# Weights of a query and a gate on 128 partitions, and a V load freed from the gate, in a one-token attention kernel

## The chip, the cores and the metric

One core of one Trainium2 chip. The time is that of one execution on the device in microseconds; lower is better. Each time is that of one execution, and each kernel has one trace, of one profiled execution.

## The reference

One token `x` of 448 values is normalized. From it come a query for 16 heads of 256 and, through a two-layer gate, a vector `g`. The query attends to a cache of 65,536 keys and values per head; the result goes through `wo` and is scaled by `g`.

```python
xn = _layernorm(x)                                   # x: 1 x 1 x 448
q  = (xn @ wq).reshape(1, 1, 16, 256)                # wq: 448 x 4096
scores = einsum("bhqd,bhkd->bhqk", q, k_cache) / 16  # k_cache: 16 x 65536 x 256
s  = einsum("bhqk,bhkd->bhqd", softmax(scores), v_cache) @ wo
g  = silu(silu(xn @ w1) @ w2)                        # w1: 448 x 1792, w2: 1792 x 448
return x + s * g
```

All is bf16. K and V are 1,074 MB, wq and wo 3.67 MB each, w1 and w2 1.61 MB each.

## The kernel before

The cache is cut into 64 blocks, each with two K tiles and two V tiles of 4.19 MB (128 partitions of 32 KB). There are two buffers for K and two for V. SyncE (SP) issues all large loads in one queue, in order, and waits ahead of each until the buffer is free:

```python
def sp_block(i):                       # i = 1 .. 63
    for t in range(2):
        take(sp, kf[t])                # DVE has read K tile t of block i-1
        sp.dma_start(out=Kt[t], in_=src(Kd, i, t)).then_inc(kl[t], 16)
        take(sp, vf[t])                # V buffer t is free
        sp.dma_start(out=Vt[t], in_=src(Vd, i - 1, t)).then_inc(vl[t], 16)
```

V lags K by one block. DVE (VectorE) and ACT (ScalarE) multiply K by the query, block after block; PE (TensorE) multiplies the softmax by V. Before the loop (cut):

```python
DC = 4; DP = D // DC                   # 448 rows on 112 partitions, four each
sp.dma_start(out=W[0:DP, 0:DC*HD], in_=A_wq.rearrange("(p c) n -> p (c n)", c=DC))
for t in range(2): ...                 # the two K tiles of block 0
w12 = Vt[1]                            # w1 and w2 lie in the second V buffer at first
sp.dma_start(out=w12[0:DP, 0:DC*F], in_=B_w1.rearrange("(p c) f -> p (c f)", c=DC))
sp.dma_start(out=w12[:, DC*F:...], in_=B_w2...)
...
for g in range(HD // 512):             # query: 8 groups of 4 matmuls
    for c in range(DC):
        pe.matmul(B, lhsT=xnT[0:DP, c, :], rhs=wq_v[0:DP, c, g*512:(g+1)*512],
                  start=(c == 0), stop=(c == DC-1))
...                                    # wo is loaded over wq
dve_block(0); act_block(0)
pe_rows()                              # waits for the end of DVE's block 0
for f in range(FC):                    # gate: 14 groups of 4 matmuls
    for c in range(DC):
        pe.matmul(ps_h[:, f:f+1], lhsT=w1_v[0:DP, c, f, :], rhs=xnT[0:DP, c, 0:1],
                  start=(c == 0), stop=(c == DC-1))
t = silu(h1s, ps_h, ...)               # ACT and DVE
for f in range(FC):
    pe.matmul(ps_y, lhsT=h1s[:, f:f+1], rhs=w2_v[:, f, :], ...)
pe.nop().then_inc(vf[0], 1)            # first V load may go
act.nop().then_inc(vf[1], 1)           # w1 and w2 are read: second V load may go
t_g = silu(g_f, ps_y, ...)             # ACT and DVE; then the loop begins
```

The first V buffer holds nothing at this time: the wait for `vf[0]` protects no data.

Of the kernel before, what the change touches and what calls it, by code (L numbers as in the profile page):

```python
# [21 lines left out]
def kernel(  # L22
# [15 lines left out]
    P = nc.NUM_PARTITIONS  # L38

    _, _, D = A_x.shape  # L40
    _, H, Sk, Dh = A_k_cache.shape
    F = B_w1.shape[1]
    HD = H * Dh
# [1 line left out]
    NB = Sk // (P * KT * TPB)  # L45
    NBLK = H * NB
    NA = SUB - ND
    DC = 4
    DP = D // DC
    assert DP * DC == D and DP <= P  # L50
    FC = F // P
    assert FC * P == F
    NHA = H * 2
# [7 lines left out]
    pe, dve, act, gp, sp = nc.tensor, nc.vector, nc.scalar, nc.gpsimd, nc.sync  # L61
# [3 lines left out]
    Vt = [pool.tile([P, KT * Dh], bf16, name=f"V{t}") for t in range(TPB)]  # L65
    W = pool.tile([P, max(DC * HD, NHA * D)], bf16, name="W")
    prod = [pool.tile([P, NA, Dh], bf16, name=f"prod{i}") for i in range(2)]
# [13 lines left out]
    ones_row = pool.tile([1, P], bf16, name="ones_row")  # L81
# [7 lines left out]
    xn = pool.tile([1, D], bf16, name="xn")  # L89
    xnT = pool.tile([P, DC, P], bf16, name="xnT")  # L90
    h1e = pool.tile([P, FC], fp32, name="h1e")
# [29 lines left out]
    def mark(e, ins):  # L121
        count[e] += 1
        ins.then_inc(line[e], 1)
        return (e, count[e])

    def need(e, *toks):
        for p, c in toks:
            if seen.get((e, p), 0) < c:
                eng[e].wait_ge(line[p], c)
                seen[(e, p)] = c  # L130

    def sem(name):
        return tc.alloc_semaphore(name)
# [7 lines left out]
    vf = [sem(f"vf{t}") for t in range(TPB)]  # L141
# [5 lines left out]
    dl = {n: sem(f"dl_{n}") for n in ("x", "wq", "w12", "wo", "out")}  # L147
# [156 lines left out]
    def pe_turn():  # L304
# [12 lines left out]
                    ins.then_inc(vf[1], 1)  # L317
        ins.then_inc(ho, 1)

    with tc.tile_critical():  # L320

        act.dma_start(out=x_f[0:1, :], in_=A_x[0, 0:1, :]).then_inc(dl["x"], 16)
        sp.dma_start(
            out=W[0:DP, 0 : DC * HD], in_=A_wq.rearrange("(p c) n -> p (c n)", c=DC)
        ).then_inc(dl["wq"], 16)
        for t in range(TPB):
            sp.dma_start(out=Kt[t][:, :], in_=src(Kd, 0, t)).then_inc(kl[t], 16)
        w12 = Vt[1]
        sp.dma_start(
            out=w12[0:DP, 0 : DC * F], in_=B_w1.rearrange("(p c) f -> p (c f)", c=DC)  # L330
        ).then_inc(dl["w12"], 16)
        sp.dma_start(
            out=w12[:, DC * F : DC * F + FC * D], in_=B_w2.rearrange("(p c) d -> p (c d)", c=FC)
        ).then_inc(dl["w12"], 16)
# [7 lines left out]
        for T, w in ((ident, P), (eye2, 2)):  # L342
            g_o = mark("gp", gp.affine_select(
                out=T[:], in_=T[:], compare_op=ALU.not_equal, fill=1.0, base=0,
# [11 lines left out]
            out=rstd[0:1, :], in_=mv[0:1, 1:2], func=ACT.Sqrt, bias=eps_t[0:1, 0:1], scale=1.0  # L356
# [5 lines left out]
            out=xn[0:1, :],  # L362
# [4 lines left out]
            op1=ALU.mult,  # L367
        ))

        xn_c = xn[0:1, :].rearrange("o (p c) -> o c p", c=DC)  # L370
        ps_xt = ps_a[:, :].rearrange("p (c n) -> p c n", c=DC)
        need("pe", t5, g_c)
        for c in range(DC):
            ins = pe.matmul(
                ps_xt[0:DP, c, :], lhsT=xn_c[0:1, c, :], rhs=ones_row[0:1, :], start=True, stop=True
            )
        t6 = mark("pe", ins)
        need("dve", t6)
        t7 = mark("dve", dve.tensor_copy(out=xnT[0:DP, :, :], in_=ps_xt[0:DP, :, :]))


        wq_v = W[:, 0 : DC * HD].rearrange("p (c n) -> p c n", c=DC)
        need("pe", t7)
        pe.wait_ge(dl["wq"], 16)
        bufs = [ps_a, ps_b]
        free = [None, None]
        for g in range(HD // 512):
            B = bufs[g % 2]
            if free[g % 2]:
                need("pe", free[g % 2])  # L390
            for c in range(DC):
                ins = pe.matmul(  # L392
                    B[:, :],
                    lhsT=xnT[0:DP, c, :],
                    rhs=wq_v[0:DP, c, g * 512 : (g + 1) * 512],
                    start=(c == 0),
                    stop=(c == DC - 1),
                )
            t8 = mark("pe", ins)
            need("act", t8)  # L400
            t9 = mark("act", act.copy(out=qb[:, g * 512 : (g + 1) * 512], in_=B[:, :]))  # L401
            free[g % 2] = t9
# [6 lines left out]
            out=W[:, 0 : NHA * D].rearrange("p (h e) -> p h e", h=H),  # L409
            in_=A_wo.rearrange("(h p a) d -> p h (a d)", p=P, a=2),  # L410
# [9 lines left out]
        w1_v = w12[:, 0 : DC * F].rearrange("p (c q f) -> p c f q", c=DC, f=FC)  # L420
        w2_v = w12[:, DC * F : DC * F + FC * D].rearrange("p (f d) -> p f d", d=D)
        ps_h, ps_y = ps_a[:, 0:FC], ps_b[0:1, 0:D]
        pe.wait_ge(dl["w12"], 32)
        need("pe", t_q)
        for f in range(FC):
            for c in range(DC):
                ins = pe.matmul(
                    ps_h[:, f : f + 1],
                    lhsT=w1_v[0:DP, c, f, :],
                    rhs=xnT[0:DP, c, 0:1],  # L430
                    start=(c == 0),
                    stop=(c == DC - 1),
                )
# [14 lines left out]
        for f in range(FC):  # L448
            ins = pe.matmul(
                ps_y, lhsT=h1s[:, f : f + 1], rhs=w2_v[:, f, :], start=(f == 0), stop=(f == FC - 1)  # L450
            )
        t = mark("pe", ins)
        pe.nop().then_inc(vf[0], 1)
        need("act", t)
        act.nop().then_inc(vf[1], 1)
        t_g = silu(g_f[0:1, :], ps_y, g_e[0:1, :], t)
# [24 lines left out]
        n = [0]  # L481

        def own(ins):
# [16 lines left out]
            out=wgt[:, :, :],  # L500
# [12 lines left out]
            out=cf[:, :, :],  # L513
# [10 lines left out]
            out=cf[:, :, :],  # L524
# [5 lines left out]
        for a in range(2):  # L530
            t = mark("dve", dve.tensor_tensor(  # L531
                out=part[:, :, a, :], in0=hv[:, :, :, 2 + a], in1=cf[:, :, :], op=ALU.mult
# [3 lines left out]
            out=OT32[:, :, :], in_=part[:, :, :, :], axis=AX.X, op=ALU.add  # L536
# [3 lines left out]
            out=OT[:, :], in_=OT32[:, :, :].rearrange("p h a -> p (h a)")  # L540
# [5 lines left out]
        for n in range(NHA):  # L546
            ins = pe.matmul(  # L547
                ps_ao[0:1, :],
                lhsT=OT[:, n : n + 1],
                rhs=wo_n[:, n, :],  # L550
                start=(n == 0),
                stop=(n == NHA - 1),
# [4 lines left out]
            out=tmp[0:1, :], in0=ps_ao[0:1, :], in1=g_f[0:1, :], op=ALU.mult  # L557
# [3 lines left out]
            out=out_bf[0:1, :], in0=tmp[0:1, :], in1=x_f[0:1, :], op=ALU.add  # L561
# [34 lines left out]
```

## Time and profile before

| | before |
|---|---|
| median of 3 runs | 2559.31 us (2557.88 to 2560.91) |
| DMA queue busy | 99% of 16 engines, 432 GB/s from 100 us on |
| DVE, PE busy | 87%, 50% |
| a block: DMA, DVE | 38.8 us, 34.5 us |

DMA is the bound nearly throughout. Only the head, the first 100 us, has anything to give, and there a chain of compute (wq, query, block 0, gate, block 1) decides when buffers come free.

### The profile page before, as it was taken

What the parts mean: (1) busy time and instruction counts of PE and PEld (TensorE: products, weight loads), DVE (VectorE), ACT (ScalarE), POOL (GpSimd) and SP (SyncE); (2) the same over time, 40 slices, a digit from 0 to 9 for tenths busy, and PEclk for the clock granted to TensorE, in tenths of its full rate; (3) what the DMA queues carried; (4) which work ended last, traced back from release to release, by engine and by line L of the source; (5) the groups of instructions that cost most, each with busy time, mean ns of one, the idle gap of its engine ahead of it and who ended that gap; (6) DMA issues with size and microseconds to landing.
All of it is one profiled execution on the core that took longest, in us unless ns stands there. A gap on an engine that the chain in (4) does not pass through costs nothing. (4 is left out here: it accounts for less than half of the span.)

```text
span 2558.7 us, 30403 instructions
## 1 busy us (share of the span) xinstructions
PE 1278.9 (50%) x4876; PEld 477.5 (19%) x4876; DVE 2218.3 (87%) x10263; ACT 1445.5 (56%) x6990; POOL 1.2 (0%) x11
## 2 busy tenths in 40 slices
PE   1554554555455445445545544554554454455456
PEld 0211211111112112112111111121121121121112
DVE  5888988988988988889889889889888898898894
ACT  4556555555655555556565555556555565655552
POOL 0000000000000000000000000000000000000000
PEclk7676777677767767776777777777777777777768
DMA  9999999999999999999999999999999999999995
GB/s 350 404 433 430 432 433 430 431 433 431 430 434 431 431 433 431 431 433 432 430 433 432 430 432 432 430 432 432 431 432 433 430 433 433 429 433 433 429 433 223
DMA packets 39343, 1084.43 MB, mean 424 GB/s; under 512 B 4162, under 2 KB 6212, under 8 KB 6212
## 3 DMA queue, kind: packets, MB, share of 16 engines
q1 hardware_dynamic: 39330, 1084.31, 99.0%
q8 instruction: 3, 0.05, 0.0%
q14 instruction: 8, 0.07, 0.0%
q10 hardware_dynamic: 2, 0.00, 0.0%
HBM read 1084.29 MB, written 0.00 MB: 424 GB/s over the span
## 5 line engine op out<-in xcount | busy, mean ns | idle before, releaser
L241 ACT ACTIVATE junk_a<-prod 128x256 bf16<-128x256 bf16 x3328 | 1330.7, 401 | 755.8 <-ACTq L136 755.8
L288 PE MATMUL psO<-V,PV 128*2 128x512 bf16 x4096 | 1169.5, 456 | 1105.8 <-PEq L136 1105.8
L206 DVE CUSTOM_DVE_ANT_0 junk_d<-K,qcur 128x256 bf16<-128x256 bf16 x4864 | 1698.8, 413 | 0.0
L288 PEld LDWEIGHTS psO<-V,PV 128*2 128x2 bf16 x4096 | 389.2, 96 | 1859.7 <-issue 1526.2
L192 DVE TENSOR_TENSOR prod<-K,qcur 128x3328 bf16<-128x3328 bf16 x256 | 482.8, 1886 | 243.5 <-DVEq L136 243.4
L241 ACT ACTIVATION_READ_ACCUMULATOR junk_a<-prod 128x1 f32 x3328 | 620.3, 186 | 0.0
L206 DVE DVE_READ_ACCUMULATOR2_ANT S<- 128x1 f32 x4864 | 365.9, 75 | 0.0
L272 ACT COPY O<-psO 2x512 f32<-2x512 f32 x64 | 36.7, 574 | 217.3 <-ACTq L136 217.3
L309 PE MATMUL ps_t<-eye,O 2*128 2x1 f32 x512 | 68.5, 251 | 49.6 <-PEq L136 49.6
L309 PEld LDWEIGHTS ps_t<-eye,O 2*128 2x128 f32 x512 | 64.9, 191 | 69.9 <-issue 69.8
L274 ACT COPY hist<-ps_t 128x2 f32 x64 | 10.2, 160 | 90.9 <-ACTq L136 90.9
L182 DVE COPY qcur<-qb 128x256 bf16 (+1 forms) x64 | 14.5, 227 | 38.6 <-ACT qb L401 23.0
L278 PE MATMUL ps_nb<-gmax,ones_row 1*128 1x1 bf16 x64 | 10.1, 158 | 62.3 <-PEq L136 62.0
L299 PE MATMUL ps_m<-ident,rmax 128*1 128x128 bf16 x64 | 14.1, 220 | 36.8 <-PEq L136 36.8
L261 ACT ACTIVATE PV<-S,hist 128x128 bf16<-128x128 f32 x64 | 25.7, 402 | 2.1
L223 DVE COPY S<-S 128x128 f32<-128x128 f32 x64 | 14.5, 227 | 9.3
L497 DVE TENSOR_REDUCE negM<-hist 128x16 f32<-128x64 f32 x1 | 0.3, 265 | 22.7 <-ACT hist L274 22.7
L171 DVE TENSOR_REDUCE gmax<-ps_m 1x1 bf16<-1x128 f32 x64 | 17.6, 275 | 1.6 <-DVEq L136 1.6
L278 PEld LDWEIGHTS ps_nb<-gmax,ones_row 1*128 1x128 bf16 x64 | 6.0, 94 | 66.2 <-issue 66.0
L224 DVE TENSOR_REDUCE rmax<-S 128x1 bf16<-128x128 f32 x64 | 18.0, 281 | 0.0
L299 PEld LDWEIGHTS ps_m<-ident,rmax 128*1 128x1 bf16 x64 | 5.4, 84 | 45.9 <-issue 37.8
L401 ACT CAST qb<-ps_a 128x512 bf16<-128x512 f32 x4 | 2.3, 585 | 18.0 <-PE ps_a L392 18.0
(55 smaller groups left out, 79.7 us busy)
## 6 DMA issues: line engine op xcount, KB each, us to landing
K<-in_A_k_cache_dram SPq DMA_DIRECT2D x128, 4096.0 KB, 21.3
V<-in_A_v_cache_dram SPq DMA_DIRECT2D x128, 4096.0 KB, 28.7
W<-in_A_wq_dram SPq DMA_DIRECT2D x1, 3584.0 KB, 17.1
W<-in_A_wo_dram SPq DMA_DIRECT2D x1, 3584.0 KB, 30.3
V<-in_B_w_dram SPq DMA_DIRECT2D x2, 1568.0 KB, 44.5
x_f<-in_A_x_dram ACTq DMA_DIRECT2D x1, 0.9 KB
out_dram<-out_bf SPq DMA_DIRECT2D x1, 0.9 KB
```

The source lines that it names most:

```text
L171: dve.reduce_max(out=gmax[0:1, :], in_=ps_m[0:1, :], axis=AX.X).then_inc(gm, 1)
L182: q_t = own(dve.tensor_copy(out=qcur[:, :], in_=qb[:, sub(q0, Dh)]))
L192: m = dve.tensor_tensor(out=prod[k % 2][:, :, :], in0=Kv[:, s * SUB + ND : (s + 1) * SUB, :], in1=qcur[:, None, :].to_broadcast([P, NA, Dh ...
L206: ins = dve.tensor_tensor_reduce(out=junk_d[jk][:, :], in0=Kv[:, s * SUB + j, :], in1=qcur[:, :], scale=1.0, scalar=0.0, op0=ALU.mult, op1 ...
L224: dve.reduce_max(out=rmax[:, :], in_=S[:, :], axis=AX.X).then_inc(rm, 1)
L241: ins = act.activation(out=junk_a[jk][:, :], in_=prod[k % 2][:, j, :], func=ACT.Identity, accum_out=S[:, a : a + 1],)
L261: act.activation(out=PV[:, :], in_=S2[:, :], func=ACT.Exp, bias=neg, scale=scale, accum_out=hist[:, at(i), 1:2].rearrange("p o s -> p (o s)"),
L272: act.copy(out=O[:, :], in_=psO[:, :]).then_inc(oc, 1)
L278: pe.matmul(ps_nb[:, 0:1], lhsT=ones_row[0:1, :], rhs=gmax[0:1, :], start=True, stop=True).then_inc(bm, 1)
L288: ins = pe.matmul(psO[:, :], lhsT=PV[:, t * KT + 2 * c : t * KT + 2 * c + 2], rhs=Vt[t][:, c * 2 * Dh : (c + 1) * 2 * Dh], start=(t == 0 a ...
L299: pe.matmul(ps_m[0:1, :], lhsT=rmax[:, 0:1], rhs=ident[:, :], start=True, stop=True).then_inc(tm, 1)
L309: ins = pe.matmul(ps_t[:, a : a + 1], lhsT=Ov[:, j, a, :], rhs=eye2[:, j : j + 1], start=(j == 0), stop=(j == 1),)
```

## The change

The intent: load wq and w1 with 128 partitions (three rows each, 384 rows) and a rest of 64 rows, since 112 partitions load slowly here (283 GB/s in the stretch of wq, beside 421 to 433 in those of the K tiles with 128); and let the first V load go at once.

```diff
-    DC = 4
-    DP = D // DC
+    DF = D // P            # 3
+    DR = D % P             # 64
+    DC = DF + 1
...
+    def load_rows(T, M, w, s):
+        sp.dma_start(out=T[:, 0 : DF*w], in_=M[0 : DF*P].rearrange("(p c) n -> p (c n)", c=DF)).then_inc(s, 16)
+        sp.dma_start(out=T[0:DR, DF*w : DC*w], in_=M[DF*P : D]).then_inc(s, 16)
+    def rows(c):
+        return slice(0, P if c < DF else DR)
...
+        sp.sem_inc(vf[0], 1)
+        load_rows(W, A_wq, HD, dl["wq"])
...
-                    lhsT=xnT[0:DP, c, :],
-                    rhs=wq_v[0:DP, c, g * 512 : (g + 1) * 512],
+                    lhsT=xnT[rows(c), c, :],
+                    rhs=wq_v[rows(c), c, g * 512 : (g + 1) * 512],
...
-                    lhsT=w1_v[0:DP, c, f, :],
-                    rhs=xnT[0:DP, c, 0:1],
+                    lhsT=w1_v[rows(c), c, f, :],
+                    rhs=xnT[rows(c), c, 0:1],
...
-        pe.nop().then_inc(vf[0], 1)
```

(The transposition of `xn` follows the same rows, and the waits count the added loads.)

More of the change, by code (lines that the diff above doesn't have):

```diff
@@ L47 @@
     NA = SUB - ND
-    DC = 4
-    DP = D // DC
-    assert DP * DC == D and DP <= P
+    DF = D // P
+    DR = D % P
+    DC = DF + 1
     FC = F // P
@@ L318, in pe_turn @@
         ins.then_inc(ho, 1)
+    def load_rows(T, M, w, s):
+        sp.dma_start(
+            out=T[:, 0 : DF * w], in_=M[0 : DF * P].rearrange("(p c) n -> p (c n)", c=DF)
+        ).then_inc(s, 16)
+        sp.dma_start(out=T[0:DR, DF * w : DC * w], in_=M[DF * P : D]).then_inc(s, 16)
+    def rows(c):
+        return slice(0, P if c < DF else DR)
     with tc.tile_critical():
         act.dma_start(out=x_f[0:1, :], in_=A_x[0, 0:1, :]).then_inc(dl["x"], 16)
-        sp.dma_start(
-            out=W[0:DP, 0 : DC * HD], in_=A_wq.rearrange("(p c) n -> p (c n)", c=DC)
-        ).then_inc(dl["wq"], 16)
+        sp.sem_inc(vf[0], 1)
+        load_rows(W, A_wq, HD, dl["wq"])
         for t in range(TPB):
@@ L328 @@
         w12 = Vt[1]
-        sp.dma_start(
-            out=w12[0:DP, 0 : DC * F], in_=B_w1.rearrange("(p c) f -> p (c f)", c=DC)
-        ).then_inc(dl["w12"], 16)
+        load_rows(w12, B_w1, F, dl["w12"])
         sp.dma_start(
@@ L368 @@
         ))
-        xn_c = xn[0:1, :].rearrange("o (p c) -> o c p", c=DC)
+        xn_c = xn[0:1, 0 : DF * P].rearrange("o (p c) -> o c p", c=DF)
         ps_xt = ps_a[:, :].rearrange("p (c n) -> p c n", c=DC)
@@ L374 @@
             ins = pe.matmul(
-                ps_xt[0:DP, c, :], lhsT=xn_c[0:1, c, :], rhs=ones_row[0:1, :], start=True, stop=True
+                ps_xt[rows(c), c, :],
+                lhsT=xn_c[0:1, c, :] if c < DF else xn[0:1, DF * P : D],
+                rhs=ones_row[0:1, :],
+                start=True,
+                stop=True,
             )
@@ L378 @@
         need("dve", t6)
-        t7 = mark("dve", dve.tensor_copy(out=xnT[0:DP, :, :], in_=ps_xt[0:DP, :, :]))
+        dve.tensor_copy(out=xnT[:, 0:DF, :], in_=ps_xt[:, 0:DF, :])
+        t7 = mark("dve", dve.tensor_copy(out=xnT[0:DR, DF, :], in_=ps_xt[0:DR, DF, :]))
         wq_v = W[:, 0 : DC * HD].rearrange("p (c n) -> p c n", c=DC)
         need("pe", t7)
-        pe.wait_ge(dl["wq"], 16)
+        pe.wait_ge(dl["wq"], 32)
         bufs = [ps_a, ps_b]
@@ L422 @@
         ps_h, ps_y = ps_a[:, 0:FC], ps_b[0:1, 0:D]
-        pe.wait_ge(dl["w12"], 32)
+        pe.wait_ge(dl["w12"], 48)
         need("pe", t_q)
```

## The prediction

Its times for the loads of 64 rows (2.4 us in the 9.7 of part (a)'s landing, some 1 us in the 4.2 of part (b), the 1.2 us lost in the sum for DMA alone) were the author's estimate; no trace had shown them.

> **What bounds the kernel now.** I read the page first, for the slices of the span and the DMA queues.
>
> ```profile
> DMA  9999999999999999999999999999999999999995
> GB/s 350 404 433 430 432 433 430 431 433 431 430 434 431 431 433 431 431 433 432 430 433 432 430 432 432 430 432 432 431 432 433 430 433 433 429 433 433 429 433 223
> ...
> q1 hardware_dynamic: 39330, 1084.31, 99.0%
> ```
>
> The 16 DMA engines are busy 99% of the time at 430 to 433 GB/s from the third slice on (a slice is 64 us). 1084.3 MB at 432 GB/s are 2510 us of a span of 2558.7. So the bound is the traffic of the K and V tiles; DVE, at 87% busy, is close behind. Only the first two slices (350 and 404 GB/s) and the last one run below this rate. The change touches the first two only, so I cut them into stretches (the view of busy time by stretches; the last two columns are the DMA share and GB/s).
>
> ```profile
> 2.00:18.20 16.20, 0.68 (x4) 0.49 (x4) 2.01 (x5) 1.58 (x2) 0.16 (x2) 1.00 1.04 283
> 18.20:36.00 17.80, 10.03 (x32) 3.55 (x32) 7.04 (x31) 9.47 (x32) 0.00 (x0) 0.86 0.98 421
> 36.00:48.00 12.00, 0.00 (x0) 0.00 (x0) 12.00 (x51) 5.84 (x31) 0.00 (x0) 0.50 0.98 300
> 48.00:58.00 10.00, 0.00 (x0) 0.00 (x0) 10.00 (x50) 6.93 (x35) 0.00 (x0) 0.50 1.12 414
> 58.00:64.50 6.50, 1.01 (x15) 0.90 (x16) 5.19 (x30) 4.89 (x20) 0.00 (x0) 0.50 0.98 423
> 64.50:74.00 9.50, 7.42 (x60) 4.13 (x58) 0.99 (x5) 0.71 (x2) 0.00 (x0) 0.60 0.64 245
> 74.00:99.00 25.00, 8.62 (x33) 2.99 (x33) 24.67 (x96) 13.10 (x65) 0.00 (x0) 0.73 1.01 433
> ```
>
> Three stretches are slow. In 2 to 18 and in 36 to 48 the engines are busy (1.04, 0.98) and yet slow (283, 300 GB/s): transfers that are inefficient in themselves. In 64.5 to 74 they are idle (share 0.64). Up to 74 us, 24.9 MB have moved (each length times its rate, summed); at 432 GB/s that is 57.6 us, so the head has lost 16.4 us.
>
> Next the SyncE queue in order of time, for which transfers these are and what holds back the next.
>
> ```profile
> 0.97 0.40 SPq L323 DMA_DIRECT2D W<-in_A_wq_dram  x1
> 1.42 0.89 SPq L327 DMA_DIRECT2D K<-in_A_k_cache_dram  x2
> ...
> 28.31 0.38 SPq L408 DMA_DIRECT2D W<-in_A_wo_dram  x1
> 46.29 3.63 SPq L165 DMA_DIRECT2D K<-in_A_k_cache_dram  x1
> 68.54 0.34 SPq L167 DMA_DIRECT2D V<-in_A_v_cache_dram  x1
> 69.14 0.33 SPq L165 DMA_DIRECT2D K<-in_A_k_cache_dram  x1
> 73.16 0.33 SPq L167 DMA_DIRECT2D V<-in_A_v_cache_dram  x1
> 95.35 0.33 SPq L165 DMA_DIRECT2D K<-in_A_k_cache_dram  x1
> ```
>
> Transfers follow the order of issue: wq in the first slow stretch; then two K tiles; w1 and w2 in the second; then wo and one K tile. Then nothing is queued until the V load at 68.54, which waits for the gate's last matmul to be reached on PE; the K load behind it (69.14) waits in the same queue. That is the idle stretch.
>
> Last, the timeline, for the compute chain beside this.
>
> ```profile
> 18.25 1.86 PE L392 MATMUL ps_a<-W,xnT 112*128 112x512 bf16 x4 [13.01 <-DMA W<-in_A_wq_dram]
> ...
> 28.93 0.23 DVE L182 COPY qcur<-qb 128x256 bf16<-128x256 bf16 x1 [22.96 <-ACT qb L401]
> ...
> 63.48 0.27 PE L299 MATMUL ps_m<-ident,rmax 128*1 128x128 bf16 x1 [35.21 <-PEq L136]
> ...
> 77.83 0.23 DVE L182 COPY qcur<-qb 128x256 bf16 x1 [0.26 <-issue]
> ```
>
> PE stands 13.01 us for wq. The query takes 10.7 us (18.25 to 28.93), DVE's first block 34.5 us (to 63.4), the gate 14.4 us (to 77.83), and only then DVE starts block 1; halfway through it, 17.5 us later, it frees the K tile that is reloaded at 95.35. No DVE operation in this chain waits for DMA once wq is there.
>
> [...] I add the times of the 128-row and the 64-row load.
>
> **The change part by part.**
>
> (a) wq, 3.67 MB. Now it is 128 rows of 24,576 B (3.15 MB) and 64 rows of 8,192 B (0.52 MB). At 432 GB/s the first is 7.3 us[...]. For start and landing I use a load into an empty queue, the V load of 68.54:
>
> ```profile
> V<-in_A_v_cache_dram SPq DMA_DIRECT2D x1, 4096.0 KB, 13.6
> ```
>
> Its 4.19 MB are 9.7 us at 432, so 3.9 us are start and landing. Landing is 0.97 + 3.9 + 9.7 = 14.6, against 18.1 (0.97 + 17.1, the page's list of DMA issues). So everything that follows wq on the compute chain moves 3.5 us earlier. The same number of matmuls runs (32 for the query, 56 for w1, by the comparison of the instruction order), with 128 rows in place of 112; [...] I give this no time. One DVE copy more (some 0.3 us, before wq is there) is hidden.
>
> (b) w1, 1.61 MB: [...] with w2 (1.61 MB, 128 rows, 3.7 us) 7.9 us in place of the 12-us stretch, in which some wo was moved too: 3 to 4 us saved. Nobody waits for w1 before 63: only DMA time.
>
> (c) The V load has its buffer free from the start, so SyncE issues it behind the K load, at some 43 to 47 us, and the next K load as soon as the first block ends (about 60). The idle stretch closes. It is worth 16 us (58 to 74) minus 5.08 MB / 432 GB/s = 11.75, so 4.25 us.
>
> **DMA alone** would gain: wq 16.2 us of the first stretch for 4.58 MB (10.6 at 432), less [...] some 0.5 of start, so about 4; w1 3 to 4; idle 4.25; 11 to 12 us in all. It does not get them, because of the next buffer. Now three tiles (V, K, V) follow the restart at 68.54: 12.58 MB, of which the stretches of 2 us show 1.72 MB by 74; the other 10.86 at 433 are 25.1 us, to 99.1. The K load at 95.35 comes before that, so DMA never notices. After the change the three tiles would be through by 99.1 - 11.5 = 87.6, but the K load of block 2 is released by DVE, whose chain moved 3.5 us only: 95.35 - 3.5 = 91.85. **DMA will run dry** for some 4 us there, and a restart costs 1.5 us (from 68.54 to 74 it moved 1.72 MB, 4.0 us' worth, in 5.46). K of block 2 effectively starts at 93.35 in place of 99.1: a gain of **5.8 us**. Behind it two tiles (K, V) cover 19.4 us, and the next K load comes 17.1 us after (112.47 - 95.35 now), so no second gap. From there both kernels stream at 432, and DVE, with 34.5 us a block against 38.8 for four tiles (16.8 MB), catches up. The gain is carried to the end: 2559.3 - 5.8 = 2553.5.
>
> Taken singly by the same working: the layout alone shifts everything by 3.5 us; the V load alone closes the idle time to 95.35 + 1.5 = 96.85, a gain of 2.3. They add.
>
> **Rivals.**
> 1. DMA's 11.5 us come through in full (2547.8). For it: 99% busy DMA. Against: the gap at 88 to 92 worked out above; it would need K of block 2 released by 87.6.
> 2. [...] 128 rows do not help because the slow start is something else (first access to memory, five transfers mixing). Then DVE's chain does not move, and only the V load pays: 2.3 us, 2557. Against it: w1 is slow too, at 300 GB/s, far from any start, and has the same 112 rows.
> 3. The early V load delays something: it precedes K of block 1's second half, which DVE needs at about 91; with 9.7 us a tile it lands near 80. Nothing is lost. Were wo or w1 behind it, the gate would wait; they are ahead of it in the queue.
> 4. The bound goes to DVE for good. No: 34.5 against 38.8 us a block; it decides one release only.
>
> **Range and chances.** Wq's landing is uncertain by 1.5 us, the restart by 1, and runs of one kernel differ by 1.5 either way (2557.88 to 2560.91). That gives 2553.5 with 2549.5 to 2557. Two per cent are 51 us, more than the whole head; nothing in the steady state is touched.
>
> **What would show it.** wq landing at 14 to 15 us (first query matmul 14.7 in place of 18.25); DVE's first copy of the query near 25.4; the first V issue before 50, the K behind it near 60; 58 to 74 us at some 430 GB/s; block 1 on DVE from 74.3; the K load of block 2 near 91.8 with a dip of DMA share just before it; 432 GB/s and the same tail thereafter. I am wrong if wq lands after 17, if no dip shows near 88 to 92, or if the steady rate moves by 1 GB/s (5.8 us).

## The result, and the profile after

The changed kernel took 2557.76 us (median of 4, 2556.17 to 2558.72) beside 2560.11 of the kernel before. A ratio is the mean time of one kernel's fast runs over that of the other's of the same rounds, so not quite the ratio of the medians: 0.9991, with an interval of 0.9974 to 1.0009. A second measurement gave 0.9998 (below). So the gain is 0.5 to 2.3 us, and not clear of noise, where 5.8 were forecast with a range down to 2.3 (2557.0); the median lies outside it.

First the stretches of the head in the kernel after (length, then busy time of PE, weight loads, DVE, ACT, GpSimd, then clock, DMA share, GB/s). The last row is from a finer cut.

```profile
2.00:18.20 16.20, 3.80 (x11) 1.03 (x11) 2.07 (x6) 2.16 (x3) 0.16 (x2) 1.00 1.03 374
...
36.00:48.00 12.00, 0.00 (x0) 0.00 (x0) 12.00 (x53) 6.49 (x32) 0.00 (x0) 0.50 1.02 356
...
64.50:74.00 9.50, 8.53 (x51) 5.21 (x51) 0.59 (x3) 0.19 (x1) 0.00 (x0) 0.51 0.98 419
74.00:99.00 25.00, 11.77 (x49) 4.22 (x47) 23.55 (x87) 12.11 (x59) 0.00 (x0) 0.73 0.71 295
...
91.00:97.00 6.00, 6.00 (x29) 2.35 (x28) 6.00 (x35) 4.47 (x23) 0.00 (x0) 1.00 0.01 5
```

All three slow stretches of the kernel before are better: 374 GB/s in place of 283, 356 in place of 300, 419 in place of 245. Summed over the prediction's stretches (length times rate; the rows cut here have 416, 431 and 449 GB/s), the changed kernel is 4.05 MB ahead at 74 us, which is 9.4 us' worth at 432 GB/s. And nearly all of it is lost again at one place: from 74 to 99 the rate is 295 where it was 433, because between 91 and 97 us next to nothing is loaded (5 GB/s, before 421). At 99 us 0.60 MB are left, 1.4 us' worth. The queue says what DMA waits for there.

```profile
1.07 0.42 SPq L321 DMA_DIRECT2D W<-in_A_wq_dram  x1
1.54 0.56 SPq L324 DMA_DIRECT2D W<-in_A_wq_dram  x1
...
45.14 0.37 SPq L165 DMA_DIRECT2D K<-in_A_k_cache_dram  x1
45.78 0.34 SPq L167 DMA_DIRECT2D V<-in_A_v_cache_dram  x1
62.23 0.33 SPq L165 DMA_DIRECT2D K<-in_A_k_cache_dram  x1
74.68 0.33 SPq L167 DMA_DIRECT2D V<-in_A_v_cache_dram  x1
96.86 0.33 SPq L165 DMA_DIRECT2D K<-in_A_k_cache_dram  x1
```

The V load goes at 45.78 in place of 68.54, as intended. The K tile of block 2 is issued at 96.86: 1.5 us later than before (95.35), where 91.85 was predicted. Its buffer is freed by DVE, halfway through block 1. So the chain, in order of time:

```profile
15.14 1.97 PE L404 MATMUL ps_a<-W,xnT 128*128 128x512 bf16 x4 [9.84 <-DMA W<-in_A_wq_dram]
...
27.77 0.23 DVE L182 COPY qcur<-qb 128x256 bf16<-128x256 bf16 x1 [21.68 <-ACT qb L413]
...
62.33 0.27 PE L299 MATMUL ps_m<-ident,rmax 128*1 128x128 bf16 x1 [35.22 <-PEq L136]
62.53 5.96 PE L439 MATMUL ps_a<-xnT,V 128*128 128x1 bf16 x56
...
79.35 0.23 DVE L182 COPY qcur<-qb 128x256 bf16 x1 [0.26 <-issue]
```

(The row of x56 merges 42 matmuls of 128 rows and 14 of 64.) Stage by stage, from these lines and those of before:

| stage | before, us | after, us | difference |
|---|---|---|---|
| first query matmul at | 18.25 | 15.14 | -3.11 |
| query, to DVE's copy | 10.68 | 12.63 | +1.95 |
| block 0 | 34.55 | 34.56 | 0 |
| gate, to DVE's next copy | 14.35 | 17.02 | +2.67 |
| half of block 1, to the K issue | 17.52 | 17.51 | 0 |
| K of block 2 issued at | 95.35 | 96.86 | +1.51 |

wq comes 3.1 us earlier, and then PE gives up 4.6 us in the query and the gate. In the gate nearly all of it is one row; in the kernel before it was

```profile
63.68 3.52 PE L427 MATMUL ps_a<-xnT,V 112*128 112x1 bf16 x56
```

The same 56 matmuls, 3.52 us before and 5.96 after. The weight loads show what is different. Kernel before, the first group of the query (PEld is a weight load; in brackets the idle time ahead of it):

```profile
18.22 0.14 PEld L392 LDWEIGHTS ps_a<-W,xnT 112*128 112x128 bf16 x2 [13.17 <-issue]
18.25 1.86 PE L392 MATMUL ps_a<-W,xnT 112*128 112x512 bf16 x4 [13.01 <-DMA W<-in_A_wq_dram]
18.63 0.15 PEld L392 LDWEIGHTS ps_a<-W,xnT 112*128 112x128 bf16 x1 [0.28 <-issue]
19.06 0.15 PEld L392 LDWEIGHTS ps_a<-W,xnT 112*128 112x128 bf16 x1 [0.28 <-issue]
19.48 0.15 PEld L392 LDWEIGHTS ps_b<-W,xnT 112*128 112x128 bf16 x1 [0.28 <-issue]
```

and the kernel after:

```profile
15.53 0.15 PEld L404 LDWEIGHTS ps_a<-W,xnT 128*128 128x128 bf16 x1 [0.28 <-issue]
16.51 0.10 PEld L404 LDWEIGHTS ps_a<-W,xnT 64*128 64x128 bf16 x1 [0.84 <-issue]
17.05 0.13 PEld L404 LDWEIGHTS ps_b<-W,xnT 128*128 128x128 bf16 x2 [0.44 <-issue]
```

Before, a weight load follows the last by 0.43 us and lies beside the matmul ahead of its own. After, the load of 64 rows stands idle for 0.84 us, and the first of 128 rows behind it for 0.44: each starts only when the matmul ahead of its own is nearly at its end (the trace's ends of matmuls are modelled). The loads themselves take no longer: in w1 0.13 us with 64 rows and 0.15 on average with 128, beside 0.16 with 112 before. From the starts of single matmuls in the trace, a group of four costs 0.86 us before and 1.07 after at PE's fast rate in the query (1.71 and 1.93 at its slow rate), and 0.24 and 0.42 in w1. (PE has two rates: in the kernel before, the 512-column matmuls follow each other by 0.43 us until 24.2 us and by 0.22 from there on. The expectations call them cold and warm, and the change to the fast one the warm-up.) So passing from 128 rows to 64 and back costs 0.18 to 0.22 us. Eight groups of the query and 14 of w1 make 8 x 0.21 + 14 x 0.18 = 4.2 us of the 4.6. For the query this is an upper estimate: part of its 1.95 us is that PE became fast later, 7.6 us after the first matmul in place of 5.9 (see r12).

That was the theory to test. The late weight loads agree with it (0.84 us idle ahead of the load of 64 rows, in place of 0.28); what in PE makes the pass cost time is not shown by any trace. The prediction had not looked for such a cost.

### The profile page after: what moved, and what is told of

It reads as the page before. It is cut to its first block, busy times and chain, and to the rows that moved or that the text cites. A ratio compares the mean times of both kernels' runs of the same rounds, so it can differ in the third digit from the quotient of the medians.

```text
span 2556.9 us, 30406 instructions
## 1 busy us (share of the span) xinstructions
PE 1283.2 (50%) x4876; PEld 478.6 (19%) x4876; DVE 2218.3 (87%) x10264; ACT 1445.4 (57%) x6990; POOL 1.2 (0%) x11
## 5 line engine op out<-in xcount | busy, mean ns | idle before, releaser
L261 ACT ACTIVATION_READ_ACCUMULATOR PV<-S,hist x64 | 11.9, 186 | 0.0
## 6 DMA issues: line engine op xcount, KB each, us to landing
W<-in_A_wo_dram SPq DMA_DIRECT2D x1, 3584.0 KB, 26.2
W<-in_A_wq_dram SPq DMA_DIRECT2D x1, 3072.0 KB, 11.5
V<-in_B_w_dram SPq DMA_DIRECT2D x1, 1344.0 KB, 34.1
W<-in_A_wq_dram SPq DMA_DIRECT2D x1, 512.0 KB, 13.5
V<-in_B_w_dram SPq DMA_DIRECT2D x1, 224.0 KB, 35.6
```

Source lines behind the costliest of these rows:

```text
L261: act.activation(out=PV[:, :], in_=S2[:, :], func=ACT.Exp, bias=neg, scale=scale, accum_out=hist[:, at(i), 1:2].rearrange("p o s -> p (o s)"),
```

## The experiments

Theory P: the passes lengthen the chain, the chain releases the K tile of block 2 late, DMA runs dry. Rivals: R, 128 rows are slower than 112 in themselves; L, the addresses of the new layout are slower to load as weights; D, DMA gives the saving back in the steady state; G, the layout is worth nothing anyway, and only the gate's place matters.

| run | median | before beside it | ratio (95%) | K of block 2 issued | last K of the loop issued |
|---|---|---|---|---|---|
| before | | | | 95.35 | 2480.69 |
| after | 2557.76 | 2560.11 | 0.9991 (0.9974 to 1.0009) | 96.86 | 2478.61 |
| r1 after again | 2558.45 | 2559.47 | 0.9998 (0.9985 to 1.0012) | 96.64 | 2478.04 |
| r2 layout only | 2562.08 | 2559.47 | 1.0008 (0.9994 to 1.0022) | 97.59 | 2482.18 |
| r3 early V only | 2557.85 | 2559.47 | 0.9994 (0.9981 to 1.0008) | 94.06 | 2478.72 |
| r4 padded | 2553.02 | 2559.47 | 0.9975 (0.9961 to 0.9988) | 90.66 | 2471.99 |
| r7 zigzag | 2555.79 | 2560.15 | 0.9982 (0.9968 to 0.9996) | 94.26 | 2475.47 |
| r8 padded, gate off | 2552.29 | 2560.15 | 0.9969 (0.9955 to 0.9983) | 80.21 | 2471.36 |
| r9 before, early V, gate off | 2558.55 | 2559.46 | 0.9996 (0.9983 to 1.0010) | 86.05 | 2477.32 |
| r10 after, gate off | 2551.74 | 2559.46 | 0.9972 (0.9958 to 0.9985) | 80.06 | 2470.99 |
| r11 padded, w1 ahead | 2552.12 | 2559.46 | 0.9970 (0.9957 to 0.9984) | 86.74 | 2471.89 |

Runs r1 to r4 shared one chip and its runs of before, so did r5 to r8, and r9 to r12. Every result was found correct, but for r5, r6 and r12 this says only that the tolerance did not notice the rows left out. These three were run once each, for their traces: 2568.69, 2560.21 and 2568.17 us.

**r1: the changed kernel again.**

> The changed kernel once more, on the chip of the next three, so that they can be compared with it. Theory P (PE pays for the pass between 128-row and 64-row matmuls, and the chain through the gate and DVE releases the K tile of block 2): 1.5 to 3 us faster than before, K of block 2 issued at 96.9 us, DMA empty for some 6 us before it. Rival D (the gain is small because DMA gives it back later, in the steady state): the rate between 100 and 2500 us is lower than in the kernel before by some 3 us' worth.

The time is 1.0 us better than before by the medians, less than the 1.5 to 3 of theory P. The trace repeats: K of block 2 at 96.64, 299 GB/s from 74 to 99. The steady state is 432 GB/s from 99 us to 2500 in both kernels, and the last K load of the loop comes 2.65 us earlier than in the kernel before. Rival D falls: what is gained at 100 us is still there at 2478.

**r2: the layout alone, and r3: the early V load alone.** In r2 the line `sp.sem_inc(vf[0], 1)` goes and `pe.nop().then_inc(vf[0], 1)` returns; in r3 the kernel before gets the opposite edit.

> The new layout alone; the V load waits for the gate again. Theory P: the first query matmul near 15.1, but the gate's second matmul group only near 69.5 (68.2 before), so the three tiles that wait for it start 1.3 us later than before and nothing else limits: 1 to 1.5 us slower than before, in spite of wq and w1 taking 7 us less DMA time. My recorded working (layout shifts the chain): 3.5 us faster. Rival D: any time between.

> The old layout with the early V load. Theory P: the chain stays as before, K of block 2 issued at 95.35, DMA empty for about 1 to 2 us before it: 2 to 2.5 us faster than before, that is, as fast as the whole change. Rival D or a rival by which the idle stretch of DMA is worth its full length: 4.25 us faster.

The queue of r2:

```profile
70.11 0.34 SPq L167 DMA_DIRECT2D V<-in_A_v_cache_dram  x1
...
97.59 0.33 SPq L165 DMA_DIRECT2D K<-in_A_k_cache_dram  x1
```

and of r3:

```profile
51.00 0.34 SPq L167 DMA_DIRECT2D V<-in_A_v_cache_dram  x1
...
94.06 0.33 SPq L165 DMA_DIRECT2D K<-in_A_k_cache_dram  x1
```

In r2 the V load goes 1.6 us later than in the kernel before, because it waits for a gate that has become slower; the last K load of the loop is 1.5 us later, and the time 2.0 us worse by the ratio, though its interval reaches 0.9994. The 3.5 us that I had recorded for the layout alone are excluded: they would be a ratio of 0.9986. In r3 the early V load gives 2.0 us at the last K load, near the 2.3 predicted for it, and the same as the whole change (2.1). That 2.3 was met is in part luck: PE became fast early in this run (3.8 us after the first query matmul, 5.9 in the kernel before), so K of block 2 went 1.3 us earlier than expected and DMA did not run dry (437 GB/s from 91 to 97). The timed runs agree that, within the noise, the V load is all of the gain in this kernel and the layout adds none.

**r4: the passes taken away.** The loads stay; the rest rows are padded with zeros on DVE, which is idle then (in the kernel before, 22.96 us ahead of its first copy of the query), and all matmuls take 128 rows.

```diff
+        dve.memset(W[DR:P, DF * HD : DC * HD], 0.0)
+        dve.memset(w12[DR:P, DF * F : DC * F], 0.0)
+        t7 = mark("dve", dve.memset(xnT[DR:P, DF, :], 0.0))
...
-                    lhsT=xnT[rows(c), c, :],
-                    rhs=wq_v[rows(c), c, g * 512 : (g + 1) * 512],
+                    lhsT=xnT[:, c, :],
+                    rhs=wq_v[:, c, g * 512 : (g + 1) * 512],
```

(and w1 likewise)

> The changed kernel with the 64-row remainder padded with zeros to 128 rows for the matmuls (the loads are unchanged), so that every matmul has 128 rows. Theory P: four query matmuls take 1.70 us cold and 0.86 warm (1.93 and 1.07 in the changed kernel), the 56 matmuls of w1 3.5 us in place of 6.0; K of block 2 issued near 93 in place of 96.9; 4.5 to 6 us faster than before, 3 to 4 faster than the changed kernel. Rival R (128 rows are slower than 112 in themselves): no change against the changed kernel.

```profile
58.32 3.52 PE L442 MATMUL ps_a<-xnT,V 128*128 128x1 bf16 x56
...
90.66 0.33 SPq L165 DMA_DIRECT2D K<-in_A_k_cache_dram  x1
```

w1 is back at 3.52 us, with 128 rows: rival R falls, and so does L, since the addresses are those of the changed kernel. The time is 5.4 us below r1's on the same chip (medians), 6.4 below before by the ratio. K went at 90.66 and not near 93 by luck of the profiled run: wq was there 0.8 us earlier (first query matmul at 14.32), and PE came to its fast rate 2.9 us after that, 7.6 in the changed kernel.

**r5, r6, r12: the passes put into the kernel before.** Only the last matmul of each group is cut, to 64 or to 96 rows, without any change of the loads.

```diff
-                    lhsT=w1_v[0:DP, c, f, :],
+                    lhsT=w1_v[0 : DP if c < 3 else 64, c, f, :],
```

(and the moving operand, and the query, likewise)

> The kernel before, in which the last of the four matmuls of each group takes 64 rows in place of 112 (wrong result on purpose: 48 rows are left out). Loads and layout are those of before. Theory P: four query matmuls go from 1.70 to 1.93 us cold and from 0.86 to 1.07 warm; w1's 56 from 3.5 to 6.0 us. Rival R (128 rows are slower than 112): no change, 3.5 us, as no matmul has 128 rows here. Rival L (the new layout's addresses make the weights slower to load): no change either.

> The same with 96 rows in place of 64 (wrong result on purpose). If any change of the number of rows costs the pass, w1 takes 6.0 us as with 64; if only a number [...] does, it takes 3.5 us as before.

With 64 rows:

```profile
68.83 5.96 PE L427 MATMUL ps_a<-xnT,V 112*128 112x1 bf16 x56
```

With 96 rows:

```profile
63.70 3.52 PE L427 MATMUL ps_a<-xnT,V 112*128 112x1 bf16 x56
```

5.96 us is the changed kernel's number to the digit, in the old layout, with less work in it. 96 rows cost nothing beside 112. So it is the pass to 64 rows and back, not a change of the count as such, and not the layout. Row counts other than 64, 96, 112 and 128 were not tried. On the whole kernel the passes do what they did in the changed one: K of block 2 is issued at 103.30 with 64 rows and at 95.14 with 96 (before 95.35), and the single runs took 2568.69 and 2560.21 us beside 2560.15 of before. One thing I had not expected: with 64 rows the query took 16.2 us (17.91 to 34.08), more than the changed kernel's 12.6, since PE stayed at its slow rate for all 32 matmuls. Was this chance?

> The kernel before with 64 rows in the last matmul of each group, once more, for TensorE's warm-up alone (wrong result on purpose). Theory W (the passes keep PE from its fast rate): again all 32 query matmuls at the slow rate, 15.7 us. Rival (chance of the moment at which the rate changes): a change to the fast rate after 3 to 8 us, as in the other runs.

It came again: eight groups at 1.9 us each, from start to start. In the kernels without passes PE became fast 2.9 to 5.9 us after its first query matmul (seven traces); with 128 and 64 mixed in groups of 3 and 1, after 3.8, 7.6, 7.6 and 9.6 us (r10, after, r1, r2). So the passes seem to delay the fast rate as well, but with 128 rows the two sets overlap, so this stays open. What the later fast rate cost can be told: r10 and r11 became fast equally early (3.8 us), and from the first query matmul to DVE's copy they took 10.93 and 9.54 us, with and without passes. So the passes alone cost the query 1.4 us, and by difference some 0.55 of the 1.95 go with the later fast rate. The clock records in the packed trace of the kernel before begin at 24.27 us, with the fast rate, and lie 6.83, 40.96, 3.41 and 13.65 us apart, multiples of 3.41; what sets the rate is not shown by any run. The profile's clock column does not show the slow rate before that: it reads 1.00 from 18.2 to 24.2 us in the kernel before, and in r5 from 14 to 34.

**r7: half of the passes.** Every second group is taken in reverse order, so that 64-row matmuls meet in pairs.

```diff
-            for c in range(DC):
+            for k, c in enumerate(range(DC) if f % 2 == 0 else range(DC - 1, -1, -1)):
```

(and start and stop by k; the query likewise)

> The changed kernel with every second group of four matmuls taken in the reverse order, so that two 64-row matmuls follow each other and half of the passes go. Theory P: w1 in 4.6 to 5.0 us (6.0 in the changed kernel, 3.5 in the kernel before), K of block 2 issued 1.5 to 2.2 us earlier than in the changed kernel (near 95), 1 to 2 us faster than it, 3 to 4 faster than before. Rival R: no change.

```profile
60.98 4.79 PE L439 MATMUL ps_a<-xnT,V 128*128 128x1 bf16 x56
```

4.79 us lies halfway between 3.52 and 5.96 (4.74), K of block 2 goes at 94.26, and the time is 4.4 us below before's, a little more than expected. The cost goes with the number of passes.

**r8, r10, r11, r9: the chain taken out of the way.** In r8 (padded) and r10 (the changed kernel, with its passes) w1's matmuls stand ahead of `pe_rows()`, where PE is idle (0.00 us busy from 36 to 58 in the kernel before), and the gate's last activation goes behind the loop. r11 does only the first of the two, padded. r9 does both in the old layout, with the early V load.

```diff
         act_block(0, first=True)
-        pe_rows()
...
         t = mark("pe", ins)          # end of w1's matmuls
+        pe_rows()
...
-        t_g = silu(g_f[0:1, :], ps_y, g_e[0:1, :], t)
+        t_y = t
...
         act_softmax(last, own)       # behind the loop
+        t_g = silu(g_f[0:1, :], ps_y, g_e[0:1, :], t_y)
```

> The padded kernel, and the gate taken off the chain to block 1: its first matmuls run on PE during block 0, and its last activation after the loop, where DVE and ACT are idle. Theory P: DVE starts block 1 near 66 to 68, K of block 2 is issued near 83 to 86, before the three tiles in front of it are through at about 90; DMA never runs dry, and the whole DMA saving arrives: 9 to 11 us faster than before. Rival D (the steady state or the tail gives it back): no more than the padded kernel's gain.

> The old layout, early V load, and the gate off the chain as in the run before. Theory P with DMA as the bound of what is left: the slow loads of wq and w1 stay (6 to 7 us), the idle stretch closes and no second one opens, since K of block 2 is issued near 85; last K load of the loop 4 to 4.5 us earlier than before, 3.5 to 4.5 us faster. If the gate's place alone made the 8 us of the padded kernel with the gate off (rival G: the layout is worth nothing even with the chain out of the way): as fast as that one, 8 us.

> The changed kernel, not padded, with the gate off the chain. Theory P: the passes between 128 and 64 rows still cost PE as much (w1 in 6.0 us, query 1.3 us or more longer), but w1 now runs in PE's idle time and block 1 starts near 64, so K of block 2 is issued near 82 and DMA never runs dry: as fast as the padded kernel with the gate off, 7.5 to 9 us faster than before. Rival R2 (the passes cost the kernel in another way than through the chain): slower than that one by 3 us or more.

> The padded kernel with only the gate's first matmuls put ahead, into PE's idle time in block 0; its last activation stays where it was. Theory P: chain 3.5 us shorter than padded alone, K of block 2 issued near 87 to 90, no dry stretch or one under 1 us; last K load of the loop 9 us earlier than before; 8 to 9 us faster than before, since the tail is left as it was (the version with the activation moved to the tail lost 1.5 to 2 us in the tail).

r10, whose PE still pays for every pass:

```profile
43.38 5.96 PE L438 MATMUL ps_a<-xnT,V 128*128 128x1 bf16 x56 [18.30 <-DMA V<-in_B_w_dram]
...
80.06 0.33 SPq L165 DMA_DIRECT2D K<-in_A_k_cache_dram  x1
...
91.00:97.00 6.00, 4.99 (x12) 1.52 (x13) 6.00 (x26) 4.21 (x21) 0.00 (x0) 0.51 1.00 427
```

The 5.96 us are there, but at 43 us, beside block 0. K of block 2 is issued at 80.06, the dry stretch of 91 to 97 now runs at 427 GB/s, and the last K load of the loop comes 9.7 us earlier than in the kernel before; the time is 7.2 us lower by the ratio. r8 and r11 are as fast within noise, so rival R2 falls: it is not PE's time that counts but its place. And r9 against r10 shows that the layout is worth something once it can arrive: with the gate off in both, 2477.32 against 2470.99 at the last K load, 6.3 us, and 2558.55 against 2551.74 in time. Rival G falls. Alone in the old layout, the gate's move and the early V load bring 3.4 us at the last K load and only 1.0 in the timed runs, less than the 3.5 to 4.5 expected.

r8, r10 and r11 too stay below what was expected of them (7.9, 7.2 and 7.7 us by the ratio, for 9 to 11, 7.5 to 9 and 8 to 9). This discrepancy is general: in nine of the ten measurements the timed difference from before, by the ratio, is 0.4 to 2.5 us worse than the difference at the last K load in the traces (the first measurement of the changed kernel agrees). The record shows two parts of it. The one trace of the kernel before is of an execution of 2560.47 us, 0.3 to 1.1 above the mean of the runs of before beside each measurement, so all differences from this trace come out too large by that; the traced execution of the other kernel lies up to 1.1 us off its own mean, either way. And the tail, from the last K load to the end, took 78.0 us in the trace of before and 78.1 to 79.8 in the others. It depends on PE's rate too: the changed kernel's matmuls on the last two V tiles took 9.84 us (granted clock 0.71) and 7.07 (1.00), before's 7.07 both (1.00).

## Why the prediction was wrong

Right, by its own steps:

- **The bound and the place of the gain.** The steady rate did not move (432 GB/s in both), and all difference arises before 100 us.
- **wq.** Landing predicted at 14.6; the rest of 64 rows landed at 15.0 (1.54 + 13.5, the after page's list of DMA issues), and the chain gained 3.1 us there for 3.5. The rest landed 2.5 us behind the 128-row part (1.07 + 11.5 = 12.6), where my estimate had been 2.4. Why the stretches with loads of 112 partitions ran at 283 GB/s (wq) and 300 (w1, with w2 in it), and 128 partitions at 421 to 433, is not shown by any run.
- **The early V load.** Issued at 45.78 (predicted 43 to 47), the idle stretch of 58 to 74 closed, and alone it brought 2.0 us at the last K load for 2.3 (r3, in part by luck).
- **The next limit.** "DMA will run dry" because DVE frees the K tile of block 2 too late: it did, and so the rival by which all of DMA's saving arrives fell. This part of the mechanism was foreseen; r10 and r11 show that it is the one that limits, since the saving arrives once the release is early.

Wrong:

- **The step that failed** is in part (a): the 128 rows in place of 112 of which it says "I give this no time." The term put at 0 measured +1.95 us in the query and +2.67 in the gate (2.44 of it in w1). With the 0.4 us of wq these are the 5.0 us between the predicted issue of K of block 2 and the measured one (91.85 and 96.86). The working had looked at the count of matmuls and even the row count 128 against 112, but not at the 64 rows that stand between them. r5 shows that these alone do it, r4 that without them it is gone. (Of the 1.95 us, 1.4 are the passes themselves and by difference 0.55 PE's later fast rate, from r10 and r11.)
- **"They add."** The two parts do not: the layout alone made the gate, and with it the V load of that kernel, later (r2), where 3.5 us were predicted.
- **w1's DMA** was put at 3 to 4 us. By the landing of wo, 58.6 before and 53.3 after (27.15 + 26.2), wq and w1 together had saved 5.3 us by then, where my terms sum to 7 or 8. It did not decide, since DMA ran dry anyway; it makes the full saving smaller than the 11 to 12 us that I had summed, and the last K load in r10 came 9.7 us earlier.

5.8 us less the 5.0 us are 0.8; the lead in bytes at 99 us is worth 1.4, the traces show 2.1 to 2.7 at the last K load, the runs 0.5 to 2.3.

## What to carry to other kernels

When a contraction is cut into pieces, count the passes between matmuls of 64 rows and of 112 or 128: each there-and-back cost some 0.2 us here (w1's 56 matmuls took 5.96 us with 64 rows in every fourth, 3.52 with 96 beside 112), and padding the rest with zeros took it away (3.52 us). Before a faster load is credited, follow the chain to the next buffer that is freed: in a kernel bound by DMA, a few microseconds on a PE that is idle half of the time (50% busy here) can decide when the next tile is issued. Work whose result is needed late (here the gate) belongs in an engine's idle time and off that chain; together with the layout and the early V load this gave 7 us, where the layout alone gave none and the gate's move and the V load without it 1.
